# A gated recurrence and a highway layer in one hand-ordered kernel: units of 768 tokens near both ends, a seventh buffer for the logits, and a new order of work

## The chip, the core and the metric

The kernel runs on one core of one Trainium2 chip. The metric is the device time of one execution in microseconds (us), as the median of several executions; lower is better. The profile is of one further execution. Its instructions are told by engine: PE is the matrix engine (PEld its weight loads), DVE the vector engine, ACT the scalar engine, POOL the GpSimd engine, SP the engine whose queue issues nearly all transfers (DMA).

## What is computed

```python
# x, f_logit: (4, 6336, 256) float32; lower_bound: (256,); w_h, w_t: (256, 256); b_t: (256,)
sig = 1 / (1 + exp(-f_logit))
f = lower_bound + (1 - lower_bound) * sig
i = 1 - f
for t in range(S):                      # along the 6,336 tokens of each sequence
    h = f[:, t] * h + i[:, t] * x[:, t]
    y[:, t] = h
X = y.reshape(25344, 256)
H = maximum(X @ w_h, 0)
T = 1 / (1 + exp(-(X @ w_t + b_t)))
out = T * H + (1 - T) * X               # (25344, 256) float32
```

## The kernel before

The 25,344 tokens are one row of *units* (`parts`, in blocks of 128 tokens): 256, 256, 512, 512, 512, then 22 units of 1,024, then 512 and 256. Each of the 29 units passes through the same steps, most of them once for each half `h` of the 256 channels. Tokens stand on the partitions when they are loaded and stored; in between the channels do, so that the recurrence is a scan along the free dimension.

The program is written out as a string, `order`. A token such as `s4.1:5` names the step (`s`), the unit (4), the half or piece (1) and the buffer (5); a `v` after the piece puts a step on DVE that otherwise is POOL's or ACT's. The tokens are emitted one after the other, and each engine keeps that order, so the string fixes the order on each engine and in SP's queue; what an instruction waits for follows from its operands and its buffer. The steps, with their lines in the profile of before:

- `l`, `x` (L256): SP loads the logits and x of a unit, up to 1 MB each. `l` and `x` have 6 buffers each (slots 0 to 5).
- `u` (L268, ACT): u = sigmoid(-logit), 16 bits, both halves in one instruction.
- `b` (L276, POOL, or DVE with `v`): bv = u * x.
- `i` (L284, PE): transposes u into PSUM, uT. `f` (L295 ACT, L293 DVE with `v`): f = 1 + ncc * uT with ncc = lower_bound - 1.
- `p` (L304, PE): transposes bv into bT. `s` (L323, DVE): the scan y = f * y + bT, carried from unit to unit. It is h divided by cc = 1 - lower_bound, and cc is folded into the weights.
- `z`, `g` (L335, and L115 for a second piece with the same weights, PE): the two products with the weights. `t` (L348, ACT): the sigmoid of z. `d` (L352, DVE): max(ncc * y, g), which is relu(X w_h) - X, since `IW` takes the identity from w_h.
- `e` (L358, POOL, or DVE with `v`): d = d * t, in up to three pieces that `ecuts` sets; units in the middle take both halves in one piece of 2,048.
- `o` (L380, L381, PE): adds diag(cc) y and d while turning them back to tokens on the partitions. `c` (L393 ACT, L391 DVE with `v`): copies the result from PSUM into the buffer `o`. `w` (L397): SP stores it, four blocks of 128 tokens (512 KB) at a time, one block at a time for the last unit; in the last units but one a copy takes two blocks.
- `k*3`: three products of zeros on PE that nothing uses (L126 the first, L115 the others), to keep PE running while there is little work. `pc`, `pb`, `cc`, `cb`, `dg` make the constants; `wh`, `wt` load the raw weights; `IW` takes the identity from w_h on POOL; `WHa`, `WTa` scale the weights on ACT.

Where a DVE instruction of step `b`, `e` or `dg` is followed in the program by one of POOL's, `shared` makes POOL's wait until DVE's has ended.

Of the kernel before, what the change touches and what calls it, by code (L numbers as in the profile page):

```python
# [19 lines left out]
def kernel(  # L20
# [37 lines left out]
b6.0:5 f6.1:2 d4.0 k*3:1 p6.1:0 s6.1:4 i6.0:1 l8:2 u7:3 z5.1:1 g5.1:2 x8:2 b7.1:6 b7.0:7 f6.0:0 t4.0 t5.1:2 i7.1:1 p6.0:0
z5.0:0 f7.1:1 d5.1:2 t5.0 o3.0:1 g5.0:2 i7.0:1 c3.0:3 s6.0:5 e5.1v w1.0 l9:3 e4.0 x9:3 w0.0 e5.2v p7.1:0 l10:4 w2.0 d5.0 e5.0
g6.0:0 z6.1:1 z6.0:2 u8:0 f7.0:3 t6.1:1 i8.0:1 e4.1v b8.0:1 b8.1:0 s7.1:6 f8.0v:2 l11:5 w3.0 t6.0 x10:4 x11:5 u9:1 d6.0:0  # L60
i8.1:0 g6.1:1 p7.0:1 s7.0:7 o5.1:2 f8.1:0 c5.1:1 o5.0:0 i9.1:0 d6.1 e6.0 p8.1:1 c5.0:0 f9.1:1 e6.2 z7.0:2 t7.0:0 o4.0:0
p8.0:0 c4.0:2 u10:2 w5.1 b9.1:3 e6.1 l12:0 w4.0 l13:1 g7.1:1 s8.1:2 i9.0:1 g7.0:2 o6.0:0 s8.0:3 i10.1:0 f9.0:3 b9.0:2 x12:0
p9.1:1 u11:3 b10.0:4 b10.1:5 b11.0:6 d7.1:2 d7.0 e7.0 z8.1:1 g8.1:2 s9.1:0 f10.1:0 p9.0:0 t8.1:2 c6.0:3 d8.1:1 i11.1:1 s9.0:1
o6.1:1 z7.1:0 f11.1:2 c6.1:1 i10.0:1 t7.1 g8.0:2 p10.0:0 z9.0:1 w6.0 w5.0 f10.0v:1 d8.0 u12:0 t9.0:1 z9.1:0 w6.1 e8.1v e7.2v
t9.1 e7.1v l14:2 x13:1 i12.1:1 f12.1:3 z8.0:2 g9.0:1 o7.1:0 s10.0:4 b11.1:7 t8.0 i11.0:1 p10.1:0 l16:3 f11.0:1 o7.0:2 u13:1
c7.0:2 d9.0:0 l15:4 e8.0 e8.2 g9.1:1 p11.0:1 s10.1:5 i13.1:0 s11.0:6 c7.1:3 f13.1:0 b12.1:0 o8.0:2 d9.1 o8.1:0 p11.1:1
i13.0:0 z10.0:1 b12.0:1 e9.0 c8.0:0 g10.0:2 s11.1:7 d10.0:2 c8.1:1 g10.1:0 f13.0:1 t10.0:0 w7.0 u14:2 w7.1 p12.1:0 z10.1:1
d10.1 z11.0:2 g11.1:0 t10.1 s12.1:2 i12.0:1 d11.1:1 t11.0:2 f12.0:2 x14:2 w8.0 w8.1 b13.1:3 z11.1:1 p12.0:0 o9.1:2 e10.0
t11.1 x15:3 l18:5 u15:3 s12.0:3 g11.0:0 p13.1:1 o9.0:1 d11.0 i14.1:0 b13.0:2 z12.0:0 c9.1:2 s13.1:0 f14.1:3 c9.0:3 o10.1:2
e11.0v x16:4 i15.1:0 p13.0:1 t12.0:1 o10.0:1 c10.1:0 f15.1:2 s13.0:1 b14.0:4 b14.1:5 c10.0:1 g12.1:0 g12.0:2 i14.0:0 w9.1  # L70
w9.0 d12.1:0 i15.0:1 d12.0 l17:0 g13.0:1 g13.1:0 z12.1:2 u16:0 f15.0:0 f14.0:1 d13.0:2 p14.0:1 b15.0:6 b15.1:7 d13.1 t12.1
w10.1 s14.0:4 w10.0 e12.0 o11.1:1 z13.0:0 u18:1 p14.1:0 o11.0:2 s14.1:5 b16.0:0 t13.0:0 x17:5 i18.0:1 l19:1 c11.1:2 w11.1
c11.0v:3 z13.1:0 f18.0:1 t13.1 g14.0:1 d14.0:1 i16.0:0 w11.0 b16.1:1 e13.0 p15.0:1 l20:2 f16.0:3 u17:2 z14.0:2 s15.0:6
o12.0:0 g14.1:1 i16.1:0 t14.0:2 b17.0:3 c12.0:0 x18:0 p15.1:1 o12.1:2 d14.1 s15.1:7 f16.1:0 w12.0 z14.1:1 c12.1:1 p16.0:0
i17.0:1 t14.1 g15.1:0 z15.0:2 w12.1 x19:1 s16.0:2 p16.1:0 f17.0:2 o13.0:1 d15.1:0 u19:3 t15.0:1 p17.0:1 o13.1:0 c13.0:2
c13.1:3 b17.1:2 e14.0 s16.1:3 z15.1:2 i17.1:0 g16.0:1 s17.0:0 g16.1:0 d16.0:2 t15.1 f17.1:3 x20:2 d16.1 u20:0 i18.1:1 z16.0:2
t16.0:0 p17.1:0 g15.0:1 z16.1:0 f18.1:0 w13.1 l21:4 b18.0:4 b18.1:5 t16.1 s17.1:1 w13.0 o14.0:2 d15.0 l22:3 i19.1:1 o14.1:0
# [20 lines left out]
e28.1 w26.1 c27.1v:3 o28.0:2 c27.0 o28.1:a1 w26.0 c28.0:2 c28.1:1 w27.0 w28.0 w28.1
"""

    NU = len(units)
# [123 lines left out]
    def scaled(k, act):  # L225
        for h in range(NH):
            if act:
                pin(nc.scalar.activation(w_sb[:, k, h], w_raw[:, k, h], AF.Copy, scale=cc[:, h:h + 1]))
            else:
                last = pin(nc.vector.tensor_scalar(w_sb[:, k, h], w_raw[:, k, h], cc[:, h:h + 1], None, op0=ALU.mult))  # L230
# [207 lines left out]
```

## Time and profile before

| | |
|---|---|
| device time, median of 3 (lowest to highest) | 206.52 us (206.36 to 206.70) |
| the profiled execution | 206.12 us, of which the span of its instructions 204.3 us |
| busy in the span | PE 189.7 us, DVE 192.9, ACT 193.0, POOL 175.5 |
| moved by DMA | 78.68 MB, mean 385 GB/s |
| granted PE clock | 0.997 |

Busy time is the union of an engine's instructions. Rows of the profile that group instructions give the count, the busy time in us, the mean duration of one in ns, and the idle time of the engine just before them with what ended it. In rows of windows each engine has its busy time with the number of instructions in brackets, and behind it stand the granted PE clock, the share of DMA time and the rate.

### The profile page before, as it was taken

The page shows a single profiled execution, that of the slowest core. Times are in us where ns is not written, and L with a number is a line of the kernel's source. Part 1 is how long each engine was busy: PE and PEld are TensorE (multiplying, and loading weights), DVE is VectorE, ACT ScalarE, POOL GpSimd, SP SyncE. Part 2 cuts the span into 40 slices and gives each one's busy share as a digit, 9 for nine tenths or more (in the row PEclk, how much of TensorE's full clock was granted, in tenths as well). Part 3 has the DMA queues.
Part 4 walks back from the last instruction along what each step waited for, and adds up shares of the span by engine and source line. Part 5 has one row for each costly group of instructions (what it writes and reads, how often), then busy time and mean ns, then how long its engine had stood idle before and what let it go on. Part 6 is the DMA issues. An engine that isn't in the chain of part 4 may idle for free. (4 is left out here: it accounts for less than half of the span.)

```text
span 204.3 us, 4632 instructions
## 1 busy us (share of the span) xinstructions
PE 189.7 (93%) x1798; PEld 132.2 (65%) x1826; DVE 192.9 (94%) x162; ACT 193.0 (94%) x201; POOL 175.5 (86%) x98
## 2 busy tenths in 40 slices
PE   7989999899899899999999999999998999999990
PEld 2455756576667757757666677676776677677680
DVE  2799999999999999999999999999999999999990
ACT  4899999999999999999999999999999999999772
POOL 3146699799996999799999979999979999989960
PEclk9999999999999999999999999999999999999998
DMA  5999999999999999999999999999999998970986
GB/s 204 347 419 422 417 419 414 411 427 419 421 424 410 431 419 419 421 419 419 427 412 425 423 420 418 419 427 422 413 359 401 426 395 306 355 287 17 396 330 242
DMA packets 16413, 78.68 MB, mean 385 GB/s; under 512 B 1796, under 2 KB 2568, under 8 KB 10760
## 3 DMA queue, kind: packets, MB, share of 16 engines
q1 hardware_dynamic: 16384, 78.39, 94.7%
q8 instruction: 14, 0.23, 0.4%
q14 instruction: 7, 0.06, 0.1%
q10 hardware_dynamic: 8, 0.00, 0.0%
HBM read 52.43 MB, written 25.95 MB: 384 GB/s over the span
## 5 line engine op out<-in xcount | busy, mean ns | idle before, releaser
L276 POOL TENSOR_TENSOR bv<-u,x 128x1024 bf16<-128x1024 f16 (+2 forms) x53 | 104.4, 1995 | 14.7 <-DVE d L358 5.7
L323 DVE TENSOR_TENSOR_SCAN y<-f,y,bT 128x1024 bf16<-128x1024 f16 (+5 forms) x56 | 106.8, 1924 | 0.2
L358 POOL TENSOR_TENSOR d<-d,t 128x512 bf16<-128x512 bf16 (+3 forms) x32 | 70.5, 2214 | 4.2 <-DVE d L358 1.8
L352 DVE SCALAR_TENSOR_TENSOR d<-y,ncc,g 128x1024 bf16<-128x1024 bf16 (+2 forms) x58 | 63.2, 1104 | 0.3 <-PE g L115 0.2
L348 ACT ACTIVATE t<-z,bt 128x1024 bf16<-128x1024 f32 (+2 forms) x58 | 61.1, 1086 | 0.8 <-PE z L115 0.8
L295 ACT ACTIVATE f<-uT,ncc 128x1024 f16<-128x1024 f16 (+2 forms) x55 | 59.7, 1097 | 0.8 <-PE uT L284 0.3
L393 ACT COPY o<-op 128x1024 f32<-128x1024 f32 (+2 forms) x53 | 51.8, 1012 | 2.3 <-ACT t L348 1.0
L268 ACT ACTIVATE u<-l 128x2048 f16<-128x2048 f32 (+2 forms) x29 | 50.7, 1750 | 2.2 <-DMA l<-in_f_logit_dram 2.2
L381 PE MATMUL op<-ident_b,d 128*128 128x128 bf16 x396 | 49.7, 219 | 0.8 <-POOL d L358 0.8
L380 PE MATMUL op<-diag,y 128*128 128x128 f16 x396 | 49.7, 219 | 0.7 <-ACT t L348 0.4
L381 PEld LDWEIGHTS <-d 128*128 128x128 bf16 x396 | 44.1, 113 | 4.5 <-POOL d L358 1.3
L380 PEld LDWEIGHTS <-y 128*128 128x128 bf16 x396 | 44.2, 113 | 2.3
L335 PE MATMUL z<-y,w_sb 128*128 128x512 bf16 (+1 forms) x114 | 39.4, 367 | 1.5 <-DVE d L352 0.3
L335 PE MATMUL g<-y,w_sb 128*128 128x512 bf16 (+1 forms) x115 | 40.1, 368 | 0.5
L304 PE MATMUL bT<-ident_f,bv 128*128 128x128 f32 x198 | 32.2, 278 | 2.9 <-DVE y L323 1.3
L284 PE MATMUL uT<-ident_h,u 128*128 128x128 f16 x396 | 31.4, 219 | 2.3 <-DVE y L323 1.6
L284 PEld LDWEIGHTS <-u 128*128 128x128 f16 x396 | 26.1, 98 | 10.8 <-issue 2.9
L335 PEld LDWEIGHTS <-w_sb 128*128 128x128 f16 x232 | 22.3, 98 | 15.7 <-ACT f L295 0.2
L304 PEld LDWEIGHTS bT<-ident_f,bv 128*128 128x128 f32 x198 | 22.1, 141 | 13.2 <-issue 4.7
L115 PE MATMUL g<-y,w_sb 128*128 128x512 bf16 x77 | 29.2, 379 | 0.0
L115 PE MATMUL z<-y,w_sb 128*128 128x512 bf16 x75 | 28.4, 379 | 0.1
L115 PEld LDWEIGHTS <-w_sb 128*128 128x128 f16 x176 | 17.2, 98 | 15.7 <-issue 1.8
(35 smaller groups left out, 53.5 us busy)
## 6 DMA issues: line engine op xcount, KB each, us to landing
out_dram<-o SPq DMA_DIRECT2D x48, 512.0 KB, 9.9
l<-in_f_logit_dram SPq DMA_DIRECT2D x22, 1024.0 KB, 14.5
x<-in_x_dram SPq DMA_DIRECT2D x22, 1024.0 KB, 15.1
l<-in_f_logit_dram SPq DMA_DIRECT2D x4, 512.0 KB, 6.4
x<-in_x_dram SPq DMA_DIRECT2D x4, 512.0 KB, 7.6
x<-in_x_dram SPq DMA_DIRECT2D x3, 256.0 KB, 3.6
l<-in_f_logit_dram SPq DMA_DIRECT2D x3, 256.0 KB, 4.0
out_dram<-o SPq DMA_DIRECT2D x2, 256.0 KB, 14.9
```

The source lines that it names most:

```text
L115: return pe.add_instruction(mybir.InstMatmult(name=nc.get_next_instruction_name(), start_tensor_calc=start, stop_tensor_calc=stop, tile_si ...
L276: shared(pin(e.tensor_mul(bv[:, :nb // 2].rearrange("p k d j -> p k j d"), st[n]["u"][:, :nb, own].rearrange("p (k j) d -> p k j d", j=2), ...
L284: pin(nc.tensor.transpose(uT[:, j * P:(j + 1) * P], st[n]["u"][:, j, h * P:(h + 1) * P], ident_h))
L295: pin(nc.scalar.activation(to, of, AF.Identity, scale=ncc[:, h:h + 1], bias=1.0))
L304: pin(nc.tensor.transpose(words[:, k:k + g * (P - 1) + 1:g], pair, ident_f))
L323: pin(nc.vector.tensor_tensor_scan(y[:, c:e], st[n]["f", h][:, c:e], st[n]["bT", h][:, c:e], 0.0 if fresh else carry[h], op0=ALU.mult, op1 ...
L335: pin(nc.tensor.matmul(p[:, a:e], w, half(n, "y", ki)[:, a:e], start=ki == 0, stop=ki == NH - 1))
L348: pin(nc.scalar.activation(half(n, "t", m), st[n]["z", m][:, :tokens(n)], AF.Sigmoid, bias=bt[:, m:m + 1]))
L352: pin(nc.vector.scalar_tensor_tensor(half(n, "d", m), half(n, "y", m), ncc[:, m:m + 1], st[n]["g", m][:, :tokens(n)], op0=ALU.mult, op1=AL ...
L358: shared(pin(e.tensor_mul(st[n]["d"][:, a:c], st[n]["d"][:, a:c], st[n]["t"][:, a:c])), not eng)
L380: pin(nc.tensor.matmul(o, half(n, "y", h)[:, cols], diag[:, h], start=True, stop=False))
L381: pin(nc.tensor.matmul(o, half(n, "d", h)[:, cols], ident_b, start=False, stop=True))
```

## The change

The number of units stays 29. The third unit of 512 tokens becomes one of 768, the last unit of 1,024 becomes one of 768, so that the row is 256, 256, 512, 512, 768, 21 of 1,024, 768, 512, 256. A unit of 768 takes its step `e` in two pieces of 768, and the stretch of units with `e` in one piece is 9 to 20 and no longer 9 to 21. The raw weights have no tile of their own any more: they lie in buffer 0 of the results (`o`), until that buffer takes its first result. The logits have a seventh buffer (slots 0 to 6). And `order` is another, from the first token to the last.

```diff
-    parts = [2] * 2 + [4] * 3 + [8] * 22 + [4] + [2]
-    ecuts = {2: (0, 256, 512), 4: (0, 512, 1024), 8: (0, 1024, 1536, 2048)}
+    parts = [2] * 2 + [4] * 2 + [6] + [8] * 21 + [6] + [4] + [2]
+    ecuts = {2: (0, 256, 512), 4: (0, 512, 1024), 6: (0, 768, 1536), 8: (0, 1024, 1536, 2048)}
...
-        units.append((nb, at, (0, 2048) if 9 <= n <= 21 else ecuts[nb]))
+        units.append((nb, at, (0, 2048) if 9 <= n <= 20 else ecuts[nb]))
...
-k*3:a0 x0:0 pc:0 l0:0 l1:1 cc u0:0 k*3:1 pb:2 i0.0:1 k*4:0 dg wh u1:1 b0.1v:0 f0.0:0 b0.0v:1 i1.0:0 x1:1 l2:2 wt IW f1.0v:1 p0.0:1
...
+l0:0 x0:0 k*3:a0 l1:1 pc:0 k*3:1 u0:0 u1:1 wh:0 IW x1:1 wt k*2:a0 i0.0:1 i0.1:0 cc f0.1:0 b0.1v:0 b0.0v:1 dg f0.0v:1 k*2:0
...
-    w_raw = sb([P, 2, NH, D], FP32, "w_raw")
+    w_raw = [None, None]
...
+    def weights(k, src, slot):
+        if "w_raw" not in once:
+            once["w_raw"] = sb([P, 4, D], FP32, "o", slot).rearrange("p (k h) d -> p k h d", h=NH)
+            w_raw[:] = [once["w_raw"][:, 0], once["w_raw"][:, 1]]
+        pin(nc.sync.dma_start(w_raw[k], src.rearrange("(h p) o -> p h o", p=P)))
```

The other lines of the diff only address the raw weights in their new place (`w_raw[k][:, h]` for `w_raw[:, k, h]`).

On DVE at the start, before: the constants, `b0.1v` and `b0.0v`, then `f1.0v`, and the scan `s0.0` ahead of the two `b` of unit 1.

```order
L217 TENSOR_SCALAR diag<-ident_h,cc 128x128 x2
L276 TENSOR_TENSOR bv<-u,x 128x2x128 x2
L293 TENSOR_SCALAR f<-uT,ncc 128x256
L207 COPY bt<-tbT 128x2
L323 SCALAR_TENSOR_TENSOR y<-f,bT 128x256
L276 TENSOR_TENSOR bv<-u,x 128x2x128 x2
```

And now, in the same place:

```order
L282 TENSOR_TENSOR bv<-u,x 128x2x128 x2
L223 TENSOR_SCALAR diag<-ident_h,cc 128x128 x2
L299 TENSOR_SCALAR f<-uT,ncc 128x256
L329 SCALAR_TENSOR_TENSOR y<-f,bT 128x256
L213 COPY bt<-tbT 128x2
L329 SCALAR_TENSOR_TENSOR y<-f,bT 128x256
```

The `f` on DVE is that of unit 0 now (`f0.0v`), so the first scan needs it, where before it needed one from ACT. The work ahead of the first scan is the same but for the copy of `bt`.

On PE at the start, with the numbers of the buffers, before: after the products of zeros the transposes of unit 0 (`u_109`, into `uT_117`), four products of zeros, the transposes of unit 1 (`u_128`) and the first `p` (`bT_148`). One row of each pair of alike rows is shown.

```order
L194 MATMUL tbT_115<-ident_f_70,tb_86 128x2
...
L284 MATMUL uT_117<-ident_h_65,u_109 128x128
...
L126 MATMUL idle_120<-zeros_61 128x512
...
L115 MATMUL idle_120<-zeros_61 128x512
...
L284 MATMUL uT_136<-ident_h_65,u_128 128x128
...
L304 MATMUL bT_148<-ident_f_70,bv_134 128x128
```

And now (`u_110` is unit 0, `u_112` unit 1, `bT_150` the first `p`):

```order
L126 MATMUL idle_121<-zeros_61 128x512
L115 LDWEIGHTS zeros_61
L115 MATMUL idle_121<-zeros_61 128x512
...
L290 MATMUL uT_124<-ident_h_65,u_110 128x128
...
L290 MATMUL uT_127<-ident_h_65,u_110 128x128
...
L126 MATMUL idle_142<-zeros_61 128x512
...
L290 MATMUL uT_145<-ident_h_65,u_112 128x128
...
L200 MATMUL tbT_148<-ident_f_70,tb_86 128x2
L310 MATMUL bT_150<-ident_f_70,bv_136 128x128
```

Two products of zeros now stand ahead of the first transposes of unit 0. The first `p` stands behind the transposes of unit 1, which are written where those of unit 0 stood (both have slot 1, in `i0.0:1` and `i1.0:1`), and so behind `f0.0v`, which reads them.

On DVE at the end, before, from the last two scans (both of unit 28) on; `d` of 1,024 is unit 26, of 512 unit 27, of 256 unit 28:

```order
L323 SCALAR_TENSOR_TENSOR y<-f,y,bT 128x256 x2
L352 SCALAR_TENSOR_TENSOR d<-y,ncc,g 128x1024
L352 SCALAR_TENSOR_TENSOR d<-y,ncc,g 128x512
L358 TENSOR_TENSOR d<-d,t 128x512 x2
L352 SCALAR_TENSOR_TENSOR d<-y,ncc,g 128x512
L391 COPY o<-op 128x512
L352 SCALAR_TENSOR_TENSOR d<-y,ncc,g 128x256
L391 COPY o<-op 128x512
L352 SCALAR_TENSOR_TENSOR d<-y,ncc,g 128x256
L391 COPY o<-op 128x512
```

And now, from the last scan on:

```order
L329 SCALAR_TENSOR_TENSOR y<-f,y,bT 128x256
L358 SCALAR_TENSOR_TENSOR d<-y,ncc,g 128x512
L397 COPY o<-op 128x512
L358 SCALAR_TENSOR_TENSOR d<-y,ncc,g 128x512
L397 COPY o<-op 128x512
L358 SCALAR_TENSOR_TENSOR d<-y,ncc,g 128x256
L397 COPY o<-op 128x512
L358 SCALAR_TENSOR_TENSOR d<-y,ncc,g 128x256
L397 COPY o<-op 128x512
L397 COPY o<-op 128x256
```

The `d` of unit 26 and DVE's last product `e` stand ahead of the last scan now, two copies more stand behind it, and DVE's last instruction is the copy of the last block of all (`c28.0v`), which was ACT's.

More of the change, by code (lines that the diff above doesn't have):

```diff
@@ L58 @@
[L58 to L77, printed above, removed]
@@ new lines @@
+t8.0:2 t8.1 s9.1:2 p9.0:0 s9.0:3 o6.0:2 g8.0:0 i10.0:1 c6.1:1 u12:0 c6.0:3 f10.0v:1 z9.1:1 p10.0:0 i11.1:1 e8.1 b11.0:6 e8.2
+t9.1:0 z9.0:2 d8.0 e8.0 g9.0:0 f11.1:3 b11.1:7 l13:0 s10.0:4 i11.0:1 t9.0 g9.1:1 e7.2 f11.0:2 w6.0 w6.1 p10.1:0 u14:1 i12.1:1
+d9.0:0 o8.0:2 o8.1:0 x13:1 d9.1 e9.0 b12.1:0 s10.1:5 b12.0:1 f12.1:1 c8.0:2 c8.1:0 u13:2 p11.0:1 s11.0:0 l15:1 p11.1:0 o7.0:1
+g10.0:2 o7.1:0 i13.1:1 c7.0:3 l16:2 s11.1:1 c7.1:1 g10.1:1 w7.0 w8.1 w8.0 f13.1:0 d10.0:2 z11.0:0 w7.1 x14:2 p12.1:0 i12.0:1
@@ new lines @@
+w11.0 i18.0:1 d13.0 c11.1:0 f18.0:2 s15.0:0 w11.1 x18:0 z14.1:1 b16.0:0 t14.1:2 g14.1:0 u17:1 d14.1:1 p15.1:1 i16.0:0 g14.0:2
+o12.0:1 f16.0:3 z14.0:0 l19:5 c12.0:2 i17.0:0 x19:1 t14.0 s15.1:1 f17.0:0 p16.0:1 z15.1:1 b16.1:1 d14.0 t15.1:0 o12.1:2
+e13.0v w12.0 i16.1:0 o13.1:0 o13.0:1 f16.1:1 e14.0v c13.1:1 p16.1:0 s16.0:6 c12.1:3 c13.0:0 g15.1:0 l20:6 i18.1:1 w12.1
+z15.0:2 f18.1:3 t15.0 s16.1:7 b17.1:3 b17.0:2 g16.0:1 i17.1:0 d15.1:0 p17.0:1 d16.0:2 s17.0:2 b18.1:4 x20:2 g16.1:0 z16.0:2
+w13.1 f17.1:1 w13.0 z16.1:1 u19:3 b18.0:5 l21:0 t16.0:1 i19.0:0 p17.1:1 o14.0:2 d16.1 l28:1 b19.0:6 g15.0:0 s17.1:3 t16.1
@@ L210, in do_IW @@
         for h in range(NH):
-            own = w_raw[:, 0, h, h * P:(h + 1) * P]
+            own = w_raw[0][:, h, h * P:(h + 1) * P]
             last = pin(nc.gpsimd.tensor_sub(own, own, ident_f))
@@ L227, in scaled @@
             if act:
[L228 removed]
+                pin(nc.scalar.activation(w_sb[:, k, h], w_raw[k][:, h], AF.Copy, scale=cc[:, h:h + 1]))
             else:
[L230 removed]
+                last = pin(nc.vector.tensor_scalar(w_sb[:, k, h], w_raw[k][:, h], cc[:, h:h + 1], None, op0=ALU.mult))
         if not act:
```

71 lines of the change are left out of this document (41 added, 30 removed).

## The prediction

> **What bounds the kernel now.** I read first the windows of the whole span: each engine's busy time in each stretch, then the share of DMA time and the rate.
>
> ```profile
> 0.00:10.00 10.00, 8.32 (x35) 3.38 (x36) 4.73 (x15) 6.13 (x11) 2.48 (x13) 1.00 0.75 272
> 10.00:20.00 10.00, 8.81 (x69) 5.32 (x69) 9.86 (x18) 9.63 (x18) 5.74 (x5) 1.00 1.03 421
> ...
> 30.00:60.00 30.00, 27.75 (x269) 19.60 (x272) 30.00 (x24) 30.00 (x28) 28.89 (x16) 1.00 1.02 419
> 60.00:90.00 30.00, 28.75 (x290) 20.88 (x293) 30.00 (x21) 30.00 (x28) 26.96 (x12) 1.00 1.02 420
> 90.00:120.00 30.00, 28.65 (x266) 19.65 (x269) 29.94 (x21) 30.00 (x28) 30.00 (x12) 1.00 1.02 420
> 120.00:150.00 30.00, 29.49 (x300) 21.60 (x305) 30.00 (x21) 30.00 (x29) 28.06 (x12) 1.00 1.02 418
> 150.00:180.00 30.00, 29.14 (x286) 21.07 (x291) 29.88 (x21) 30.00 (x31) 28.38 (x13) 1.00 0.96 368
> 180.00:190.00 10.00, 9.95 (x103) 7.36 (x104) 9.82 (x8) 8.80 (x11) 9.88 (x8) 1.00 0.41 164
> 190.00:204.30 14.30, 9.42 (x112) 7.18 (x110) 8.79 (x14) 8.45 (x15) 7.31 (x7) 0.96 0.82 318
> ```
>
> The columns are PE, PEld, DVE, ACT, POOL. From 10 to 190 us DVE and ACT do not stop, and until 150 us the DMA engines do not either. Nothing in the middle waits, so the time is DVE's work, plus what DVE stands idle at both ends: 5.27 us in the first ten, 5.51 in the last stretch. ACT is as full, so work taken from ACT and given to DVE does not help; it lengthens the one that decides. So I ask three things: how much work DVE has after the change, how its start moves, and how soon after its last instruction the program ends.
>
> **The change part by part.** The sum is made against the profiled execution, 206.12 us (its span of 204.3 and 1.8 around it); that is 0.4 below the median of 206.52.
>
> *DVE's work.* I counted the steps with their engine and size in both orders. Their durations are in the groups of instructions by shape:
>
> ```profile
> L293 DVE TENSOR_SCALAR f<-uT,ncc 128x1024 f16<-128x1024 f16 x2 | 2.5, 1256 | 0.0
> L358 DVE TENSOR_TENSOR d<-d,t 128x2048 bf16<-128x2048 bf16 x4 | 5.3, 1356 | 0.0
> L358 DVE TENSOR_TENSOR d<-d,t 128x1024 bf16<-128x1024 bf16 x1 | 0.7, 680 | 0.0
> L358 DVE TENSOR_TENSOR d<-d,t 128x512 bf16<-128x512 bf16 x13 | 5.1, 425 | 0.1
> L276 DVE TENSOR_TENSOR bv<-u,x 128x512 bf16<-128x512 f16 x1 | 0.7, 728 | 0.0
> L391 DVE COPY o<-op 128x1024 f32<-128x1024 f32 x1 | 1.2, 1186 | 0.0
> L391 DVE COPY o<-op 128x512 f32<-128x512 f32 x3 | 2.1, 691 | 0.4 <-PE op L381 0.2
> L323 DVE TENSOR_TENSOR_SCAN y<-f,y,bT 128x1024 bf16<-128x1024 f16 x38 | 88.2, 2334 | 0.2
> L323 DVE TENSOR_TENSOR_SCAN y<-f,y,bT 128x512 bf16<-128x512 f16 x8 | 10.0, 1272 | 0.0
> ```
>
> Two more `f` of 1,024: +2.51 us. Products `e`: 1 to 5 of 1,024 (+2.72), 13 to 5 of 512 (-3.40), 4 to 3 of 2,048 (-1.36). One more `b` of 512: +0.73. Copies: the one of 1,024 goes (-1.19), one of 512 comes (+0.69), and one of 256, estimated at 0.4 from the row for 512. Scans and `d`: two of 1,024 and two of 512 become four of 768 each; on the line between the two scan rows that is no change (four at 1.80 for 7.21 before). Sum **+1.1**; one instruction fewer in all, and each begins about 0.08 before the one ahead of it has ended, so **+1.2** (0.9 to 1.5 for the 768s, which no row shows). By the same counts ACT loses about 2 us, which buys nothing while DVE is full.
>
> *POOL's work.* It is beside the path as long as it fits.
>
> ```profile
> L276 POOL TENSOR_TENSOR bv<-u,x 128x1024 bf16<-128x1024 f16 x44 | 95.0, 2187 | 8.3 <-DVE d L358 5.7 <-ACT u L268 2.1 <-issue 0.4
> L276 POOL TENSOR_TENSOR bv<-u,x 128x512 bf16<-128x512 f16 x7 | 8.1, 1168 | 6.4 <-DVE bv L276 4.8 <-PE g L335 1.5
> L358 POOL TENSOR_TENSOR d<-d,t 128x1024 bf16<-128x1024 bf16 x8 | 17.5, 2185 | 1.8 <-ACT t L348 0.9 <-DVE d L358 0.6 <-DVE d L352 0.3
> L358 POOL TENSOR_TENSOR d<-d,t 128x512 bf16<-128x512 bf16 x13 | 15.0, 1162 | 1.9 <-DVE d L358 1.2 <-PE uT L284 0.8
> ```
>
> `b`: two of 1,024 and three of 512 fewer, four of 768 (1.68 on the line) more: -1.2. `e`: four of 1,024 fewer, six of 512 and four of 768 more: +4.9. Together +3.7. From 30 to 180 us POOL is busy 142.3 of 150, so it has 7.7 to give and keeps 4: cost 0. If that cover were gone, scans would wait for `b`, each for up to one POOL instruction (2.2).
>
> *The start.* The next view is the timeline of DVE and PE up to the first scan; ACT's first row shows what it waited for.
>
> ```profile
> 4.16 0.63 ACT L268 ACTIVATE u<-l 128x512 f16<-128x512 f32 x1 [1.30 <-DMA l<-in_f_logit_dram]
> 4.83 0.77 DVE L276 TENSOR_TENSOR bv<-u,x 128x256 bf16<-128x256 f16 x2
> 4.45 0.97 PE L115 MATMUL idle<-zeros 128*128 128x512 bf16 x2
> 5.36 0.22 PE L194 MATMUL tbT<-ident_f,tb 2*128 2x2 f32 x1
> 5.85 0.81 PE L115 MATMUL idle<-zeros 128*128 128x512 bf16 x3
> 6.49 0.28 PE L284 MATMUL uT<-ident_h,u 128*128 128x128 f16 x2
> 6.75 0.33 PE L304 MATMUL bT<-ident_f,bv 128*128 128x128 f32 x1
> 6.81 0.48 DVE L293 TENSOR_SCALAR f<-uT,ncc 128x256 f16<-128x256 f16 x1 [1.20 <-PE uT L284]
> 7.27 0.68 DVE L323 TENSOR_TENSOR_SCAN y<-f,bT 128x256 bf16<-128x256 f16 x1
> ```
>
> Before, the first scan begins at 7.27, behind `f` on DVE. Now the products of zeros of the second `k*3` still end at 5.42 (4.45 + 0.97), and two more stand ahead of the transposes of unit 0: 0.97 at the slow rate of that row, 0.54 at the rate of the row at 5.85. Then transposes (0.28), `f0.0v` (0.48), and, because the transposes of unit 1 overwrite what `f0.0v` reads, one after the other the transposes of unit 1 (0.28), the bias (0.22) and the first `p` (0.33). With 0.1 of handovers the scan begins at 5.42 + 0.54 to 0.97 + 1.59 + 0.1, between 7.65 and 8.1, which is 0.4 to 0.8 later, with the same work done before it. That `l0` is issued ahead of `x0` brings `u0` forward (ACT waited 1.30 for it), but the chain begins at PE's zeros at 5.42, later than `u0` is done already (4.79). I take **+0.5**; bounds 0 (later gaps that before had up to 20 us go instead) and +1.0 (0.8 and a wait for the first `t`).
>
> *The end.* Timelines of the last instructions, then windows of one us.
>
> ```profile
> 198.50 0.69 DVE L391 COPY o<-op 128x512 f32<-128x512 f32 x1 [0.24 <-PE op L381]
> 198.94 1.07 ACT L393 COPY o<-op 128x512 f32<-128x512 f32 x2 [0.41 <-ACT t L348]
> 200.35 0.37 ACT L393 COPY o<-op 128x256 f32<-128x256 f32 x1 [0.34 <-DMA out_dram<-o]
> 188.00:189.00 1.00, 1.00 (x6) 0.45 (x5) 0.82 (x2) 0.94 (x2) 1.00 (x2) 1.00 0.15 57
> 197.00:198.00 1.00, 1.00 (x18) 0.96 (x16) 0.89 (x3) 0.64 (x2) 1.00 (x2) 1.00 1.01 401
> 198.00:199.00 1.00, 1.00 (x19) 0.85 (x16) 0.76 (x2) 0.59 (x3) 0.58 (x2) 1.00 1.02 410
> 202.00:203.00 1.00, 0.00 (x0) 0.00 (x0) 0.00 (x0) 0.00 (x0) 0.00 (x0) 1.00 0.53 176
> ```
>
> DVE ends at 199.19, 5.1 us before the span's end. ACT's last copy ends at 200.72, 3.6 before. But the DMA engines are full from 197 on and still move data at 202.5: what ends last is the queue of stores, and unit 27's 512 KB decide, whose copies end at about 199.5, 4.8 before the end. Now the copy of unit 27 on DVE is followed only by the last copy of all (0.4), so DVE's end lies 4.4 before the span's end instead of 5.1: **-0.7** (-1.5 if the queue is not what ends last and only the 3.6 behind the last copy remain). And DVE loses time by waiting: 0.18, 0.11 and 0.24 in the three windows shown, 0.05 in others, and at each of five waits the 0.08 of overlap: 1.0. In the new order `d`, `c`, `d`, `c` alternate without `e`, and POOL's and PE's work for each copy is a step ahead; I leave 0.1: **-0.9** (-1.0 to 0).
>
> *With one answer.* The seventh buffer of logits lets loads be issued sooner, but the queue runs at 419 GB/s and ACT waits for logits only in the first six us: 0; a load pushed behind one more store of 512 KB would come 1.25 us later (0.524 MB at 419 GB/s), which the depth of the queue hides. The raw weights in a result buffer: the first copy into it stands behind the scaling of the weights on the same engine, 0. Twenty products of zeros instead of 27: PE has room from 10 us on, 0.
>
> A rule that speaks against the change is weighed on two rows from the middle:
>
> ```profile
> 148.71 1.80 DVE L358 TENSOR_TENSOR d<-d,t 128x2048 bf16<-128x2048 bf16 x1
> 145.12 4.31 POOL L276 TENSOR_TENSOR bv<-u,x 128x1024 bf16<-128x1024 f16 x2
> ```
>
> This product began while POOL still ran, to 149.43, and took 1.80, where the other three have 1.21 (4 x 1.356 less 1.80, by three). The Trainium skill (SBUF — State Buffer, Terms) says that DVE and GpSimd arbitrate for a shared pair of ports which is exclusive for a whole instruction, so that the loser is blocked entirely. By that rule it would have ended at 149.43 + 1.21 = 150.64; it ended at 150.51, so the trace nearly agrees, and the sum would grow by the rest of POOL's instruction for each such meeting.
>
> **Sum:** 1.2 + 0.5 - 0.7 - 0.9 = +0.1. On the scale of the median 206.52 that is **206.6 us**: no change that can be told. A measurement of this kernel can tell about 0.2% (0.4 us) from no change.
>
> **The rivals.** *The end is shorter than I say (faster).* Unit 26 now has 768 tokens, so 256 KB fewer wait in the queue behind the last copies, 0.6 us at 410 GB/s. If the queue is through in time, the end shrinks by 1.5, and if the zeros run at the fast rate the start costs 0.2: 1.2 + 0.2 - 1.5 - 0.9 = -1.0, **205.5**. For it: ACT's last copy itself waited for a store, 0.34. Against it: the full windows from 197 on.
>
> *DVE's products meet POOL (slower).* DVE has eight long products (five of 1,024, three of 2,048) instead of five, and POOL's idle time falls from 7.7 to 4. One meeting more with half of a POOL instruction left costs 1.1: **207.7**. It decides from one more meeting on. Against it: only one of five shows it before.
>
> *The start costs twice (slower).* DVE's first products now stand right behind `t` of the same units. If DVE waits there twice for 0.3 on top of 0.5: **207.2**.
>
> *PE stays slow (slower).* With two zeros between the small steps of the start, PE may keep the slow rate, 0.49 for a product of zeros against 0.27. About 2 us of PE work on the chain up to 10 us would take 1 more: **207.6**. The Trainium skill (TensorE: Matmul & The Clock Gate, Part 1) lets the clock drop to half after an idle window of about 3.4 us; the granted clock is 1.00 in every row here, so only the two rates above could speak for that.
>
> **How the numbers follow.** Forecast 0.37, with 206.1 to 206.9 as its own range. The shorter end 0.31. Products meeting POOL 0.14, the start costing twice 0.14, PE slow 0.04. So faster by over 0.2% 0.31, within 0.37, slower 0.32. The range takes in the shorter end and all of the slower cases but their tails: 205.4 to 207.7.
>
> **What would show it.** Right: DVE busy 1.2 more and ACT about 2 less; the first scan at 7.6 to 8.1; no wait of DVE between 20 and 180; DVE's last instruction within 4.5 of the end. Wrong: DVE waiting for ACT or PE in the middle, a long product near 2 us beside a POOL row, or a DMA queue that is idle when the last copy ends.

## The result and the profile after

| | before | after |
|---|---|---|
| median, us | 206.67 (205.99 to 207.41, 11 runs) | 207.39 (206.90 to 207.93, 11 runs) |
| after over before | | 1.0040, 95% interval 1.0026 to 1.0053 |
| profiled execution, its span, us | 206.12, 204.3 | 207.68, 205.9 |

The change makes the kernel slower by 0.8 us (0.5 to 1.1). The forecast was +0.1 (206.6), with a range up to 207.7. The two profiled executions lie further apart than the medians, by 1.6, and this difference will have to be explained first.

The first line of the page gives each engine's busy time. It was DVE 192.9, ACT 193.0, POOL 175.5 before.

```profile
PE 192.0 (93%) x1827; PEld 132.8 (64%) x1827; DVE 195.0 (95%) x161; ACT 191.9 (93%) x198; POOL 179.0 (87%) x103
```

The windows of the changed kernel, in the columns that the prediction named (PE, PEld, DVE, ACT, POOL):

```profile
0.00:10.00 10.00, 8.44 (x33) 3.47 (x34) 4.11 (x14) 5.63 (x11) 2.49 (x13) 1.00 0.80 296
10.00:20.00 10.00, 8.43 (x70) 5.10 (x69) 9.71 (x17) 9.73 (x16) 3.75 (x3) 1.00 1.02 421
...
120.00:150.00 30.00, 29.07 (x284) 20.39 (x283) 30.00 (x21) 30.00 (x29) 30.00 (x11) 1.00 1.02 421
150.00:180.00 30.00, 29.20 (x302) 21.45 (x301) 29.99 (x21) 29.03 (x30) 27.96 (x16) 1.00 0.92 358
180.00:190.00 10.00, 9.87 (x97) 6.89 (x95) 10.00 (x8) 9.50 (x12) 10.00 (x8) 1.00 0.60 237
190.00:205.90 15.90, 11.34 (x142) 9.14 (x140) 11.30 (x16) 8.40 (x14) 10.13 (x10) 0.95 0.64 249
```

DVE is full from 20 to 190 us, as before; ACT now has gaps from 150 on. In the last stretch DVE is idle for 4.60 us, where it was 5.51.

The start, as the timeline of PE and DVE shows it. The two products of zeros run at the slow rate (0.63 each, against 0.38 at the fast one), and the first scan begins at 7.86:

```profile
5.31 0.63 PE L126 MATMUL idle<-zeros 128*128 128x512 bf16 x1
5.73 0.63 PE L115 MATMUL idle<-zeros 128*128 128x512 bf16 x1
6.16 0.54 PE L290 MATMUL uT<-ident_h,u 128*128 128x128 f16 x4
6.53 0.38 PE L126 MATMUL idle<-zeros 128*128 128x512 bf16 x1
7.86 0.69 DVE L329 TENSOR_TENSOR_SCAN y<-f,bT 128x256 bf16<-128x256 f16 x1 [0.77 <-PE bT L310]
```

Two of DVE's products begin well before one of POOL's has ended, where before there was one such meeting (either kernel has one more that costs less than 0.2). The rows of DVE are `e21.0v` and `e25.0v`, of 1,024 columns each; a row of POOL stands ahead of each:

```profile
168.49 2.27 POOL L364 TENSOR_TENSOR d<-d,t 128x512 bf16<-128x512 bf16 x2
169.94 1.35 DVE L364 TENSOR_TENSOR d<-d,t 128x1024 bf16<-128x1024 bf16 x1
191.01 2.29 POOL L364 TENSOR_TENSOR d<-d,t 128x512 bf16<-128x512 bf16 x2
192.70 1.16 DVE L364 TENSOR_TENSOR d<-d,t 128x1024 bf16<-128x1024 bf16 x1
```

POOL ends at 170.76 and 193.30; DVE's products end at 171.29 and 193.86, each 0.53 to 0.56 later. Where POOL is quiet such a product takes 0.67 (below), so DVE loses 0.68 and 0.49. Before, `e19.0v` lost 0.58 (1.80 against 1.22).

The end, in the timelines of DVE, ACT and POOL and in windows of one us:

```profile
199.87 0.48 DVE L358 SCALAR_TENSOR_TENSOR d<-y,ncc,g 128x256 bf16<-128x256 bf16 x1 [0.16 <-PE g L341]
201.64 0.37 ACT L399 COPY o<-op 128x256 f32<-128x256 f32 x1 [0.25 <-PE op L387]
200.49 0.67 POOL L364 TENSOR_TENSOR d<-d,t 128x256 bf16<-128x256 bf16 x1 [0.34 <-DVE d L358]
201.82 0.42 DVE L397 COPY o<-op 128x256 f32<-128x256 f32 x1 [0.76 <-PE op L387]
200.00:201.00 1.00, 0.78 (x14) 0.60 (x12) 0.98 (x2) 0.45 (x2) 0.66 (x2) 1.00 0.60 229
203.00:204.00 1.00, 0.00 (x0) 0.00 (x0) 0.00 (x0) 0.00 (x0) 0.00 (x0) 1.00 0.96 352
```

DVE's last copy ends at 202.24, 3.64 us before the end (the span is 205.89). Before, ACT's last copy ended 3.62 before the end (204.34). The DMA engines move data behind the last copy too (0.96 of full from 203 to 204), so their share alone does not say whether that copy or the queue of stores decides. The profiles of all fourteen runs of this case do: from the last copy, on whichever engine, to the end it is 3.60 to 3.66 us in every one, and from the last copy of unit 27, by which the prediction reckoned, 4.49 to 5.03.

What the last copy waits for goes round all engines: PE's last products waited 0.44 for POOL's last product, this one 0.34 for the `d` of unit 28 on DVE (199.87), and that one 0.16 for PE. The chain of work that ended last, followed back from there to 190 us, runs on PE almost throughout.

**The difference of the two profiles in one sum.** DVE's idle time up to 25 us is 5.51 before and 6.17 after; from 25 to 190 us 0.36 and 0.14; behind its last instruction 5.15 and 3.64; waits between 190 us and that instruction 0.40 and 0.94. Its busy time grew by 2.1, of which 0.6 is the meetings. So: work +1.5, meetings +0.6, start +0.66, waits after the start +0.32, end -1.5, together +1.6.

### The profile page after: what moved, and what is told of

Same layout as the page of the kernel before. It is cut to its first block, busy times and chain, and to the rows that moved or that the text cites. A ratio compares the mean times of both kernels' runs of the same rounds, so it can differ in the third digit from the quotient of the medians.

```text
span 205.9 us, 4667 instructions
## 1 busy us (share of the span) xinstructions
PE 192.0 (93%) x1827; PEld 132.8 (64%) x1827; DVE 195.0 (95%) x161; ACT 191.9 (93%) x198; POOL 179.0 (87%) x103
## 4 chain that ended last, share of the span: by engine, by line
PE 51%; DVE 19%; ACT 16%; issue 7%; POOL 3%; DMA 1%; POOLq 0%; ACTq 0%; DVEq 0%
DVE y L329 13%; PE g L341 7%; PE op L387 7%; PE op L386 7%; PE bT L310 7%; PE z L341 6%; PE uT L290 6%; PE g L115 6%; PE z L115 5%; DVE d L358 4%; ACT t L354 4%; ACT f L301 4%; ACT u L274 4%; ACT o L399 3%; POOL bv L282 2%
## 5 line engine op out<-in xcount | busy, mean ns | idle before, releaser
L282 POOL TENSOR_TENSOR bv<-u,x 128x1024 bf16<-128x1024 f16 (+3 forms) x52 | 102.8, 2001 | 15.3 <-ACT t L354 6.8
L329 DVE TENSOR_TENSOR_SCAN y<-f,y,bT 128x1024 bf16<-128x1024 f16 (+6 forms) x56 | 108.2, 1947 | 0.1
L364 POOL TENSOR_TENSOR d<-d,t 128x512 bf16<-128x512 bf16 (+4 forms) x38 | 75.6, 2005 | 2.5 <-DVE d L358 1.1
L358 DVE SCALAR_TENSOR_TENSOR d<-y,ncc,g 128x1024 bf16<-128x1024 bf16 (+3 forms) x58 | 63.3, 1106 | 0.3 <-PE g L341 0.2
L354 ACT ACTIVATE t<-z,bt 128x1024 bf16<-128x1024 f32 (+3 forms) x58 | 58.1, 1035 | 2.8 <-PE z L341 1.6
L301 ACT ACTIVATE f<-uT,ncc 128x1024 f16<-128x1024 f16 (+3 forms) x53 | 54.9, 1043 | 1.9 <-PE uT L290 1.7
L399 ACT COPY o<-op 128x1024 f32<-128x1024 f32 (+2 forms) x52 | 49.5, 994 | 2.6 <-PE op L387 1.9
L274 ACT ACTIVATE u<-l 128x2048 f16<-128x2048 f32 (+3 forms) x29 | 49.8, 1716 | 1.6 <-DMA l<-in_f_logit_dram 1.6
L341 PE MATMUL g<-y,w_sb 128*128 128x512 bf16 (+1 forms) x116 | 40.6, 368 | 1.6 <-DVE y L329 0.8
L341 PE MATMUL z<-y,w_sb 128*128 128x512 bf16 (+1 forms) x116 | 40.3, 368 | 0.9 <-DVE y L329 0.6
L115 PE MATMUL z<-y,w_sb 128*128 128x512 bf16 (+1 forms) x92 | 34.0, 370 | 0.0
L115 PE MATMUL g<-y,w_sb 128*128 128x512 bf16 (+1 forms) x92 | 34.0, 370 | 0.0
```

The costliest lines, as they stand in the source:

```text
L115: return pe.add_instruction(mybir.InstMatmult(name=nc.get_next_instruction_name(), start_tensor_calc=start, stop_tensor_calc=stop, tile_si ...
L282: shared(pin(e.tensor_mul(bv[:, :nb // 2].rearrange("p k d j -> p k j d"), st[n]["u"][:, :nb, own].rearrange("p (k j) d -> p k j d", j=2), ...
L301: pin(nc.scalar.activation(to, of, AF.Identity, scale=ncc[:, h:h + 1], bias=1.0))
L329: pin(nc.vector.tensor_tensor_scan(y[:, c:e], st[n]["f", h][:, c:e], st[n]["bT", h][:, c:e], 0.0 if fresh else carry[h], op0=ALU.mult, op1 ...
L341: pin(nc.tensor.matmul(p[:, a:e], w, half(n, "y", ki)[:, a:e], start=ki == 0, stop=ki == NH - 1))
L354: pin(nc.scalar.activation(half(n, "t", m), st[n]["z", m][:, :tokens(n)], AF.Sigmoid, bias=bt[:, m:m + 1]))
```

## The experiments

In each, the comparison is with runs of the kernel before on the same chip; the changed kernel stands at 1.0040 and 207.39 us on that scale.

| run | what is changed | median, us | over before, 95% interval |
|---|---|---|---|
| e1_nozeros | after, two products of zeros less | 207.37 | 1.0023 (1.0002 to 1.0043) |
| e2_lock | after, `e22.2` behind `e21.0v` | 207.36 | 1.0029 (1.0008 to 1.0049) |
| e3_f_back | after, `f22.1` back on ACT | 207.64 | 1.0030 (1.0009 to 1.0050) |
| e4_l7 | before, with the change's buffers | 207.02 | 1.0011 (0.9989 to 1.0034) |
| e5_b_head | before, another head | 206.81 | 1.0025 (1.0002 to 1.0048) |
| e6_b_lock | before, `e19.0v` behind `d20.0` | 207.44 | 1.0035 (1.0019 to 1.0051) |
| e8_cold | after, ten products of zeros less | 208.45 | 1.0090 (1.0064 to 1.0115) |
| e9_swap | after, `e25.0v` behind `s28.0` | 207.93 | 1.0057 (1.0036 to 1.0079) |
| e10_b_2f | before, two `f` on DVE | 208.60 | 1.0082 (1.0060 to 1.0103) |
| e11_nz_swap | after, e1 and e9 together | 207.68 | 1.0047 (1.0029 to 1.0065) |
| e12_c28 | after, `c28.0` on ACT | 207.48 | 1.0038 (1.0022 to 1.0054) |

Diffs are pieces of the lines of `order`.

**More work on DVE.**

```diff
-f14.1:3
+f14.1v:3
-f22.1:2
+f22.1v:2
```

> The kernel before, in its own order, with two f of 1,024 (f14.1 and f22.1) on DVE instead of ACT, the same two as in the changed kernel: 2.36 us more of DVE's work and about 2.0 less of ACT's. Theory (DVE sets the time): 1.7 to 2.4 us above the kernel before; 1.7 if e19.0v, which comes later by one f, no longer meets POOL's b23.1. Rival (ACT binds as much as DVE, or DVE's later waits take it up): under 0.8 above.

Measured: +1.7 us (1.2 to 2.1) by the ratio, +1.9 by the medians. DVE's busy time rose by 2.3, and the meeting of `e19.0v` with POOL stayed, since POOL's row moved with it:

```profile
PE 191.3 (92%) x1826; PEld 132.2 (64%) x1826; DVE 195.2 (94%) x164; ACT 192.0 (93%) x199; POOL 175.6 (85%) x98
144.74 6.38 POOL L276 TENSOR_TENSOR bv<-u,x 128x1024 bf16<-128x1024 f16 x3
150.40 1.79 DVE L358 TENSOR_TENSOR d<-d,t 128x2048 bf16<-128x2048 bf16 x1
```

The theory holds, at the low end: work put on DVE lengthens the program by most of its size, and ACT's relief (its busy time fell by 1.0, half of what was expected) does not make up for it. These are the same two `f` that the change moves.

**Less work on DVE.**

```diff
-f22.1v:2
+f22.1:2
```

> The changed kernel with one f of 1,024 (f22.1) given back from DVE to ACT: 1.18 us less of DVE's work, about 1.2 us more of ACT's. Theory (DVE alone sets the time): 0.8 to 1.2 us below the changed kernel's. Rival (ACT is as full as DVE): no change within 0.3, with DVE's waits for t or g grown by about 1 us behind 160 us.

Measured: no gain, the rival's side (its waits were to come behind 160 us; they come at 149). The timeline of DVE shows two new waits, together 1.72, for the 1.18 that was taken away:

```profile
148.90 0.88 DVE L329 TENSOR_TENSOR_SCAN y<-f,y,bT 128x320 bf16<-128x320 f16 x1 [0.78 <-PE bT L310]
154.54 2.35 DVE L329 TENSOR_TENSOR_SCAN y<-f,y,bT 128x1024 bf16<-128x1024 f16 x1 [0.94 <-ACT o L399]
```

So DVE's work is a bound, but not the only one: PE, and ACT with `f22.1` back on it, had less in hand at this place than the 1.18 that DVE was given. Read with the run above, more work costs at once, and less work pays only if the others are ahead.

**The meetings.** Three attempts to take one away, two on the changed kernel and one on the kernel before. (`e21.0v` takes 1.35 in the changed kernel, as shown above; the first expectation puts it at 1.31.)

```diff
-e22.1 e22.2 t23.1:2
+e22.1 t23.1:2
-e21.0v d23.0:1
+e21.0v e22.2 d23.0:1
```

> The changed kernel with POOL's product e22.2 moved behind DVE's product e21.0v in the order, so that the two do not run side by side. Theory (a product on DVE that begins while POOL's product runs is held until POOL's has ended, and DVE keeps the loss): e21.0v takes 0.60 to 0.70 us instead of 1.31, and the time is 0.5 to 0.8 us below the changed kernel's. Rival (the long time of e21.0v is slack that the end takes up): e21.0v is as short, but the time falls by less than 0.2. Third: another of POOL's instructions takes the place and the meeting stays, no change.

Measured: 207.36, no change, the third case. `e21.0v` took 0.67, and the loss turned up at the next products, `e23.1v` and `e23.0v`: POOL, which had waited for `e21.0v`, now ran beside them. The two took 0.99 together in the changed kernel and 1.78 here, so DVE was relieved of nothing:

```profile
169.22 0.67 DVE L364 TENSOR_TENSOR d<-d,t 128x1024 bf16<-128x1024 bf16 x1
173.18 2.17 POOL L282 TENSOR_TENSOR bv<-u,x 128x1024 bf16<-128x1024 f16 x1
174.45 1.78 DVE L364 TENSOR_TENSOR d<-d,t 128x512 bf16<-128x512 bf16 x2
```

In the kernel before:

```diff
-f22.0:1 e19.0v l24:0 o18.0:1 w17.1 i22.1:0 g20.0:2 c18.0:1 f22.1:2 i23.1:1
+f22.0:1 g20.0:2 l24:0 i22.1:0 f22.1:2 o18.0:1 w17.1 c18.0:1 d20.0 e19.0v i23.1:1
-f23.1:3 d20.0 p22.0:0
+f23.1:3 p22.0:0
```

> The kernel before with its one meeting taken away: e19.0v moved one step back on DVE, behind d20.0, by which time POOL's b23.1 has ended (g20.0 and i22.1 go ahead of o18.0 on PE and f22.1 ahead of c18.0 on ACT, so that d20.0 is ready). Theory of the lock: e19.0v takes 1.20 to 1.25 instead of 1.80, POOL's next product starts no later, and the time is 0.4 to 0.7 below the kernel before. Rival (DVE waits for g20.0, or ACT loses 0.5 that it does not get back): no gain, within 0.2.

Measured: 1.0035, so not faster but slower by 0.7 (0.4 to 1.1). The product took the 1.22 that was expected, and the scan behind it waited 0.69 for ACT, on which the copy and `f22.1` had changed places:

```profile
151.17 1.22 DVE L358 TENSOR_TENSOR d<-d,t 128x2048 bf16<-128x2048 bf16 x1
153.07 2.35 DVE L323 TENSOR_TENSOR_SCAN y<-f,y,bT 128x1024 bf16<-128x1024 f16 x1 [0.69 <-ACT o L393]
```

In the last ten us of the changed kernel:

```diff
-t27.1:1 e25.0v g26.0:1 o25.2:2 s28.0:0 g27.1:a0
+t27.1:1 g26.0:1 s28.0:0 e25.0v o25.2:2 g27.1:a0
```

> The changed kernel with e25.0v moved behind s28.0 on DVE, to where POOL waits for ACT's t26.0 anyway, and o25.2, which reads its result, behind both on PE. Theory of the lock: e25.0v takes 0.60 to 0.70 instead of 1.16, DVE's last instruction ends 0.3 to 0.5 earlier, and the time is 0.3 to 0.5 below the changed kernel's 207.39. Rival (in the last ten us DVE is one engine of four on the path): the product is short, DVE waits as much longer for g28 or op28, and the time falls by less than 0.2.

Measured: 207.93, not less than the changed kernel. The product took 0.67, and the rest is as the rival said: by 195.3 DVE has lost what it won, by a wait for PE, and POOL's last chain begins 0.25 later, since it now waits for this product. The time of DVE's last copy, which waits 0.76 in both kernels, did not come forward:

```profile
193.43 0.67 DVE L364 TENSOR_TENSOR d<-d,t 128x1024 bf16<-128x1024 bf16 x1
194.25 6.16 POOL L364 TENSOR_TENSOR d<-d,t 128x768 bf16<-128x768 bf16 x5 [0.95 <-DVE d L364]
195.32 0.75 DVE L329 TENSOR_TENSOR_SCAN y<-f,y,bT 128x256 bf16<-128x256 f16 x1 [0.23 <-PE bT L310]
202.07 0.42 DVE L397 COPY o<-op 128x256 f32<-128x256 f32 x1 [0.76 <-PE op L387]
```

An earlier edit, e7_swap, moved `e25.0v` behind `s28.0` but left `o25.2` ahead of both. PE then adds a value that has not been multiplied yet, so that kernel computes something else, and its 208.85 (1.0102) says nothing of this question.

What a meeting costs DVE is thus shown five times over (the product ends when POOL's instruction has ended and its own time has passed); the Trainium skill (SBUF — State Buffer, Terms) states this as an exclusive port pair, and the rows agree: each product ends 0.11 to 0.15 before POOL's end plus its own 0.67, 0.99 or 1.22. What a meeting costs the program is not shown: in e2_lock it only moved, and in e6_b_lock and e9_swap it was gone, but other waits came in its place and the time did not fall.

**The start.**

```diff
-wt k*2:a0 i0.0:1
+wt i0.0:1
```

> The changed kernel without the two products of zeros that stand on PE between the weights' load and the first transposes. Theory (DVE is full from its first scan to its end, so what it loses at the start is kept to the end): the first scan begins at 7.0 to 7.4 us instead of 7.86, DVE's last instruction ends 0.5 to 0.8 earlier, and the time is 0.5 to 0.8 us below the changed kernel's. Rival (ACT or POOL are as full, and a lead of DVE is given back in waits for them further on): the first scan is earlier by the same, but DVE waits 0.5 or more for ACT or POOL before 100 us, and the time falls by less than 0.3.

Measured: the median is that of the changed kernel, the ratio 0.0017 lower, less than the two intervals can tell apart. The first scan came at 6.83 (in e11_nz_swap, which has the same head, at 7.50), but the last copy waited 1.04 for a store to free its buffer:

```profile
6.83 0.69 DVE L329 TENSOR_TENSOR_SCAN y<-f,bT 128x256 bf16<-128x256 f16 x1 [0.79 <-PE bT L310]
201.53 0.42 DVE L397 COPY o<-op 128x256 f32<-128x256 f32 x1 [1.04 <-DMA out_dram<-o]
```

Inconclusive in size. But the runs that left the head alone showed why the start was misread. Three timelines: the changed head again in e12_c28 and e2_lock, where products of zeros take 0.38 to 0.39, the fast rate, at 4.06 and 4.91 already, and the old head again in e4_l7, with the slow rate until past 6.2:

```profile
4.06 0.39 PE L126 MATMUL idle<-zeros 128*128 128x512 bf16 x1
```

```profile
4.91 0.38 PE L126 MATMUL idle<-zeros 128*128 128x512 bf16 x1
7.13 0.69 DVE L329 TENSOR_TENSOR_SCAN y<-f,bT 128x256 bf16<-128x256 f16 x1 [0.99 <-PE bT L310]
```

```profile
5.83 0.63 PE L126 MATMUL idle<-zeros 128*128 128x512 bf16 x1
6.25 1.07 PE L115 MATMUL idle<-zeros 128*128 128x512 bf16 x3
7.95 0.68 DVE L329 TENSOR_TENSOR_SCAN y<-f,bT 128x256 bf16<-128x256 f16 x1
```

PE's rate rises somewhere between 4.1 and 6.7 us, differently in each execution of the same head, and the first scan moves with it. In both heads the arrival of `l1` moves it as well: `u1`, which waits for it, began at 5.71 in the profile of before and at 6.73 in that of e6_b_lock, and in e9_swap the rate was fast by 5.7 but the transposes of unit 1 waited for `u1` until 7.12. The old head has its first scan at 7.27, 7.95, 8.21 and 7.92 (before, e4, e6, e10), the new one at 7.86, 7.13, 7.88, 7.86 and 6.72 (after, e2, e3, e9, e12). DVE's idle time up to 25 us is 5.51, 6.07, 6.48 and 6.10 in the old head (mean 6.04), and 6.17, 5.44, 6.10, 6.07 and 5.15 in the new one (mean 5.79). (The head of e7_swap is the new one too, with 6.16; with it the mean is 5.85.) So the new head costs -0.25 on the average, give or take 0.3 (each head scatters by 0.4), which is not told apart from nothing, and not +0.66: the profile of before had caught the best of its four starts, that of after the worst of its five. With -0.25 in place of +0.66 the sum of the last section gives +0.7, and the medians say +0.72.

The profiled times bear this out. Each is one run of its kernel, and over these nine it lies off the median of that kernel as its start does: 0.70 and 0.55 us below it where DVE was idle for 5.15 and 5.51, 0.62 above where it was 6.48. A line through all nine, each head taken from its own mean, gives 0.9 us of time for one us of start (the two profiles of e1_nozeros's head, 5.27 and 5.79, do not show it). So a start that is late for all engines at once appears to be kept to the end, unlike a stall of DVE alone.

> The kernel before, in its own order, with the change's seventh buffer of logits and the raw weights in the first result buffer alone. Theory: no change from the kernel before, within 0.3 us, since ACT waits for logits only in the first six us. Rival (loads issued sooner collide with stores): 0.4 to 1.0 us slower.

The edit of this run is the seventh slot in the numbers of `l`, and `weights` in a result buffer as in the change. Measured: 1.0011 (0.9989 to 1.0034), not told apart from none: a median 0.33 higher, at the edge of what was expected.

Without the ten products of zeros that follow the first three:

```diff
-l0:0 x0:0 k*3:a0 l1:1 pc:0 k*3:1 u0:0
+l0:0 x0:0 l1:1 pc:0 u0:0
-wt k*2:a0 i0.0:1
+wt i0.0:1
-f0.0v:1 k*2:0
+f0.0v:1
```

> The changed kernel without the ten products of zeros that PE computes ahead of unit 0's work (three of those at the program's very start stay). Theory (PE's rate rises at its own time, and the zeros only stand in the way): the first scan begins at 5.9 to 6.5 instead of 7.1 to 7.9, and the time is 0.6 to 1.5 below the changed kernel's. Rival (PE's rate rises only after some us of unbroken products, and without them it stays slow into the first units' work): transposes and products for g take twice as long up to 10 us or more, DVE waits for them between 8 and 20 us, and the time is the same or up to 1.5 above.

Measured: 1.0 us above the changed kernel (by the ratios), the size that the rival gave. The zeros are what brings the fast rate on: with them it is there by 6.7 us at the latest, without them a product still took the slow rate's 0.63 at 8.31, and the first scan gained nothing:

```profile
7.27 0.69 DVE L329 TENSOR_TENSOR_SCAN y<-f,bT 128x256 bf16<-128x256 f16 x1 [1.47 <-PE bT L310]
8.31 0.63 PE L126 MATMUL idle<-zeros 128*128 128x512 bf16 x1
202.14 0.42 DVE L397 COPY o<-op 128x256 f32<-128x256 f32 x1 [1.10 <-DMA out_dram<-o]
```

The waits that the rival put between 8 and 20 us are small, 0.61 of DVE's time against 0.29 in the changed kernel. DVE loses 0.5 more in the last ten us, where its last copy waits for a store to free its buffer. How the slow start leads there is not shown; this profile is of the fastest of the six runs.

Where the zeros keep PE busy, the rise thus comes 2.9 to 5.5 us after PE's first product (at 1.19). The Trainium skill (TensorE: Matmul & The Clock Gate, Part 1) says about 4 us of sustained work, give or take 0.5 from run to run; these 4 us lie inside the range seen here, which is more than twice as wide as the page's.

For the old head, another order:

```diff
-pb:2 i0.0:1 k*4:0 dg wh u1:1 b0.1v:0 f0.0:0 b0.0v:1 i1.0:0 x1:1 l2:2 wt IW f1.0v:1 p0.0:1
-WHa cb i0.1:0 s0.0:0 f0.1:2 x2:2
+pb:2 i0.0:1 i0.1:0 dg wh b0.1v:0 f0.0:0 b0.0v:1 f0.1:2 u1:1 x1:1 l2:2 wt IW p0.0:1
+WHa cb s0.0:0 i1.0:0 f1.0v:1 x2:2
```

> The kernel before with another head: the four products of zeros behind the first transposes are gone, i0.1, f0.0 and f0.1 stand ahead of u1, and i1.0 and f1.0v behind s0.0, so that the first scan no longer hangs on the second load of logits. Theory (PE's products of zeros at the slow rate and the order around them set the first scan, and DVE keeps every tenth of it to the end): the first scan begins at 6.4 to 7.0, against 7.27 and 7.95 in the two profiled runs of that head, and the time is 0.4 to 0.9 below the kernel before. Rival (DVE then waits for the loads of x1, l2 and x2 instead): the first scan is as early, but DVE's waits up to 20 us take it back, within 0.2.

Measured: the first scan at 6.97, within what was expected, and no gain: 1.0025. PE was at the slow rate for its transposes, four in 0.61, and the scan waited for it. DVE's idle time up to 25 us is 5.61, 0.43 below the mean of the old head, but three products near 62 us, 1.23 together in the profile of before, took 1.62, since the first began beside a row of POOL:

```profile
5.64 0.61 PE L284 MATMUL uT<-ident_h,u 128*128 128x128 f16 x4
6.97 0.69 DVE L323 TENSOR_TENSOR_SCAN y<-f,bT 128x256 bf16<-128x256 f16 x1 [1.07 <-PE bT L304]
60.25 2.12 POOL L358 TENSOR_TENSOR d<-d,t 128x1024 bf16<-128x1024 bf16 x1
61.71 1.62 DVE L358 TENSOR_TENSOR d<-d,t 128x512 bf16<-128x512 bf16 x3
```

The twelve times fall in two groups, six from 206.25 to 206.62 and six from 207.00 to 207.95; the profile, 206.62, is of the lower one, so it does not show what lengthens the upper one.

**Both cheap repairs together.**

> The changed kernel with both of its cheap repairs: without the two products of zeros ahead of the first transposes, and e25.0v with o25.2 behind s28.0. Theory (losses of DVE add up): the sum of the two alone, 0.5 to 1.0 below the changed kernel's 207.39, so 206.4 to 206.9, level with the kernel before. Rival (each loss taken away is lost again further on): less than 0.3 below the changed kernel.

Its edit is that of e1_nozeros and that of e9_swap. Measured: 207.68, the rival's case: no gain over the changed kernel. Neither had gained alone what was expected of it, so this does not test whether losses add up.

**The end.**

```diff
-c28.0v:3
+c28.0:3
```

> The changed kernel with the last copy but one, c28.0, back on ACT behind c28.1, so that DVE ends with c27.1 at about 200.9. Theory (the end is a fixed time, some 3.6 us, after the last copy, on whichever engine that runs): no change, within 0.3, with 5 us or so between DVE's last instruction and the end. Rival (the end follows DVE's last instruction): 0.7 to 1.3 us less.

Measured: 207.48, 1.0038: no change, as the theory has it. DVE ends at 200.17 and ACT's last copy at 201.40, 3.6 before the end of that span, 205.0:

```profile
199.48 0.69 DVE L397 COPY o<-op 128x512 f32<-128x512 f32 x1
200.75 0.65 ACT L399 COPY o<-op 128x256 f32<-128x256 f32 x2 [0.25 <-PE op L387]
```

So it buys nothing to have the last copy on DVE. Behind 190 us DVE now waits 0.18 and stands idle for 4.82 after its last instruction, 5.00 together; in the changed kernel the two are 0.94 and 3.64, and the copy itself 0.42, 5.00 again.

None of the eleven beats the kernel before, and none points to one that would.

## Why the prediction was right or wrong

- **No change that can be told: not so.** The time rose by 0.8, twice what can be told. 207.39 lies outside the forecast's own range (206.1 to 206.9) and inside the wide one, which took in the slower rivals. DVE as the engine that decides was right as far as added work goes (e10_b_2f) and wrong where it said that DVE alone decides (e3_f_back, e6_b_lock, e9_swap).
- **DVE's work, +1.2 (0.9 to 1.5): right, at its upper end.** Busy time rose by 2.1; without the meetings it is +1.5. ACT's fell by 1.1, not 2.
- **POOL's work, +3.7: measured +3.5.** No scan of DVE waits for `b` in the middle, so the cover held as priced; what came with the fuller POOL was the second meeting.
- **The start, +0.5: the mechanism was right for that execution and the term is wrong.** The first scan at 7.86 lies within 7.65 to 8.1. But it was set against one execution of before whose start was a lucky one. Over nine profiles the term is -0.25, give or take 0.3: well below +0.5, and about at the lower bound of 0.
- **The end, -0.7: mis-sized, -1.5.** The end follows the last copy by 3.60 to 3.66 us on either engine, not the copies of unit 27: the bound of -1.5 that was named was the value. But counted as a gain it was wrong: e12_c28 gives the last copy back to ACT, and the time stays.
- **DVE's waits, -0.9: this step failed.** It left 0.1; the waits after the start are 0.76 before and 1.08 after, +0.3. The last copy alone waits 0.76, for PE, which waits for POOL's last product, and so on round the engines; in the last ten us PE is on the path at least as much as DVE. The sentence that POOL's and PE's work for each copy is a step ahead is what is wrong.
- **The rival of the products that meet POOL came about**, with two meetings instead of one, but at 0.7 and 0.5, not 1.1, and its price for the program could not be shown. The shorter end came about too, and was used up by the rest. The start did not cost twice. PE's slow rate goes, with the arrival of `l1`, into the scatter of both starts; that it makes the difference of the kernels is not shown. (The granted clock is 0.96, not 1.00, in the last of the rows of before.)
- **The seventh buffer and the weights in a result buffer: 0**, not contradicted by e4_l7.

Together, forecast and measured: work +1.2 and +1.5, meetings 0 and +0.6, start +0.5 and -0.25, waits -0.9 and +0.3, end -0.7 and -1.5: +0.1 and +0.7. That the sum is off by no more than 0.6 is luck: start and end came out 0.75 and 0.8 lower than forecast, waits, meetings and work 1.2, 0.6 and 0.3 higher. This is an account of DVE's time. Which part of the +0.7 would go if one term were repaired stays open: of the repairs tried, e2_lock, e6_b_lock and e9_swap each brought back a loss of about the same size or more. A repair that leaves the order of the other engines as it is was not found.

## What to carry to other kernels

Where four engines are busy for over 85% of the time in one hand-made order, work added to the fullest one costs most of its size, but a stall taken away returns as another engine's stall within a few us: price what is added, and do not count on what is removed until a run has shown it. A term that is read from the first ten us of one execution against another's needs several profiles of each: here the start of one and the same head scatters by 1.2 us, more than the change is worth. At the end, count from the last copy of any engine, and ask what that copy waits for.

## What was not expected of the hardware

PE's rate doubles (0.42 to 0.22 us from one product of 512 columns to the next) at a moment that varied between 4.1 and 6.7 us over executions of the same head; the granted clock of these ten us reads 1.00 all the same. The rise came after 8.3 us where ten of the first products of zeros were left out, and that program was 1.0 us slower. A product `e` on DVE that began while POOL ran was held until POOL's instruction had ended, each time, and in e2_lock, where POOL was shifted, the hold moved to the next products.
